# Hash attention into a gated product: inversions, bit transfers and the last pair's steps put in another order

## The chip, the cores and the metric

The kernel runs on one core of a Trainium2 chip. The metric is the device time of one execution in microseconds (us); of several runs the median is taken. A core has five engines that work side by side: TensorE (PE; its weight loads are shown apart as PEld), VectorE (DVE), ScalarE (ACT), GpSimd (POOL) and SyncE (SP). Each takes its instructions strictly in the order in which the program gives them, and semaphores tie the engines together. DMAs are issued by SP, ACT or POOL and land later.

## What is computed

The first half is attention with a mask by hash buckets, for 4 x 8 heads of 768 positions and 64 features; the second half takes the heads side by side as 3072 tokens of 512 features:

```python
q_bits, k_bits = (q @ proj > 0), (k @ proj > 0)        # 6 bits each
mask = bucket(q_bits) == bucket(k_bits)
scores = where(mask, q @ k.T / 8, -1e9)
attn = exp(scores - max); attn = attn / (sum(attn) + 1e-9)
x = attn @ v                                            # heads side by side: 3072 x 512
h = maximum(x @ w_in, 0)                                # w_in 512 x 2048
out = (h * h) @ w_out                                   # w_out 2048 x 512
```

The inputs come as 64-bit floats for the weights of the second half where the host gives them so; the kernel turns such words into 32-bit floats itself.

## The kernel before, in words

**Stages.** Heads are taken two at a time: 16 pairs, numbered 0 to 15, in the loop at L729. After the pairs comes a short seam (L858 to L873), then the product with `w_in`, the gate and the product with `w_out` for three chunks of 1024 tokens (from L1494). These products are split by Strassen's scheme (seven products for eight, twice nested in parts), so VectorE has many additions beside TensorE's work. `hidden` (L988) makes one unit of the first chunk: seven sums of four matmul instructions each in `product` (L890), with copies of partial results by ScalarE (`keep`, L904) and gates by VectorE (L985, L976). Its copies go to buffers of limited number, `KEPT` in L888: `two` has one.

**A pair.** The whole order is written out by hand (`tc.manual_schedule()`), so what stands first in the text stands first in each engine's queue. There are six key tiles of 128 keys and two halves of the queries. `score(pr, kt, i)` (L463) is a step of TensorE: matmuls of the hash bits (`bits`, bf16) that put a huge negative number where buckets differ, and matmuls of features (`feat`), in one of two PSUM tiles that are used in turn (`turn`, L103); ScalarE takes the exponential from it (`weight`, L458) into a ring of four tiles (`key_of`, L444). `attend(pr, kt, s)` (L513) multiplies such a tile with the values into the PSUM tile `xo`. Scores and attends alternate, and the attends of the last key tiles of a pair run beside the first scores of the next (`beside`). In `attend` the two halves of TensorE's rows write different banks; when they change over, `part` (L499) puts a fence between: a no-operation on POOL's queue that waits for the last matmul before and releases the first one after. The fence so waits behind whatever POOL has queued before it. A pair has such fences at `attend(pr, 0, 1)`, `attend(pr, 2, 0)` and `attend(pr, 4, 1)`; the last of these, here the fourth values' fence, falls into the next pair's start.

**Totals.** VectorE adds the six exponential tiles up (`add_up`, L485). TensorE sums over the keys by matmuls with ones (`sum_up`, L554, into PSUM tile `tot`), for two pairs together in each odd pair (`sums_and_hashes`, L581); the same place holds the hashes of the next two pairs (`hash_bits`, L373, and `signs`, L398, on ScalarE). VectorE then turns and inverts them (`invert`, L597: transpose, reciprocal, copy), ScalarE copies them across (`spread`, L613: four small copies), VectorE spreads them over the positions and scales the values (`normalize`, L620), and SP stores the result to DRAM. Before that, ScalarE has copied the values out of `xo` (`keep_x`, L535). An odd pair inverts for pair pr - 2, behind `add_up(pr, 1)` and `part_power`; an even pair inverts for pair pr - 2 near its start.

**Bits.** The signs of a pair are scaled on ScalarE (`weigh`, L405) and moved into place by eight DMAs on POOL's queue (`place_bits`, L412). Both stand in the middle of the pair before the one that needs them: `weigh` before `score(pr, 3, 0)` and `place_bits` behind `attend(pr, 0, 1)`.

**Weights.** Each pair also rounds one piece of the weights: `part_power` (VectorE), `place_power` (ScalarE, four small steps), `part_top` and `round_weight` (VectorE, two instructions each), then SP stores it. From pair 4 on some pairs add pieces of `w_in` for the later scheme (`sum_in`, L653), as many as L677 says, each with stores on SP.

**The start** fills TensorE with matmuls on nothing (`keep_busy`, L354) until the first inputs are there. **The seam** adds the last total, sums it, inverts, makes the subtractions of the first chunk (`sum_x`, L701), does the last values (`attend_whole`, L529) and normalizes.

Of the kernel before, what the change touches and what calls it, by code (L numbers as in the profile page):

```python
# [34 lines left out]
def kernel(  # L35
# [318 lines left out]
    def keep_busy(n):  # L354

        wide = busy.rearrange("p (o n) -> p o n", o=1).to_broadcast([P, 4, P])
        for _ in range(n):
            nc.tensor.matmul(
                out=void[:, 0].rearrange("p (o n) -> p o n", o=4), lhsT=busy, rhs=wide,
                start=True, stop=True,  # L360
            )
# [219 lines left out]
    def sums_and_hashes(prs, nexts):  # L581

        if not nexts:
            return sum_whole(prs)
        new_totals(prs)
        sum_up(prs[0], 0)
        for n, nxt in enumerate(nexts):
            hash_bits(nxt, turn("hash"))  # L590
            signs(nxt)
            if n < len(prs):
                sum_up(prs[n], 1)
            if n + 1 < len(prs):
                sum_up(prs[n + 1], 0)

    def invert(pr):  # L597

        flip = p_n.tile([P, HS], FP32, name="flip")
        nc.vector.transpose(  # L600
            out=flip.rearrange("p (c f) -> p c f", c=2), in_=spares.pop(pr)
        )
        once = p_n.tile([P, NB], FP32, name="once")
        nc.vector.reciprocal(
            out=once, in_=flip.rearrange("p (n f) -> p n f", f=32)[:, :, 0]
        )
        rec = p_n.tile([P, 2, NB], FP32, name="rec")
        nc.vector.tensor_copy(
            out=rec, in_=once.rearrange("p (o n) -> p o n", o=1).to_broadcast([P, 2, NB])
        )  # L610
        onces[pr] = once, rec
# [64 lines left out]
    for pr in range(NIN, NP):  # L676
        n = 1 + pr % 2  # L677
        sums[pr], todo = todo[:n], todo[n:]
# [29 lines left out]
    with tc.manual_schedule():  # L708
# [3 lines left out]
        keep_busy(6)  # L712
# [16 lines left out]
        for pr in range(NP):  # L729
# [12 lines left out]
            if pr == 0:  # L742
                first_score()
                first_keys(1, spare("hash"))
            else:
                score(pr, 0, 0)
                attend(old, 4, 0)
                score(pr, 0, 1)
                attend(old, 5, 0)
                add_up(old, SB - 1)  # L750
                if not odd:
                    invert(pr - 2)
                if pr == 1:
                    features(3)
                    part_top(0)
                round_weight(old)
                if later:
                    later.pop(0)()
                if more:
                    load_weight(pr + 1)  # L760
                for m in sums.get(pr, ()):
                    sum_in(m)
            score(pr, 1, 0)
            beside(4, 1)
            score(pr, 1, 1)
# [4 lines left out]
            else:  # L770
                keep_x(old)
                if odd:
                    sums_and_hashes(
                        range(max(pr - 2, 0), pr), [n for n in (pr + 1, pr + 2) if n < NP]
                    )
            add_up(pr, 1)
# [4 lines left out]
            part_power(pr)  # L781
            if odd and pr > 1:
# [3 lines left out]
            score(pr, 2, 0)  # L786
            if odd:
# [4 lines left out]
            if pr > 0:  # L792
                if pr > 1:
                    spread(pr - 2)
# [3 lines left out]
                if more:  # L798
                    weigh(pr + 1)
                else:  # L800
                    place_power(pr, 0, 0)
# [8 lines left out]
            if more:  # L810
# [11 lines left out]
            if not more:  # L822
                invert(old)
# [11 lines left out]
            if not more:  # L835
                spread(old)
                normalize(old)
# [4 lines left out]
            if 0 < pr < NP - 1:  # L842
# [14 lines left out]
            add_up(pr, 4)  # L857
        pr = NP - 1  # L858
        attend(pr, 2, 0)
        attend_whole(pr, SB - 2)  # L860
        add_up(pr, SB - 1)
        sum_whole((pr,))
        invert(pr)
        for n in (1, 2, 3):
            sum_x(0, n)
        spread(pr)
        attend_whole(pr, SB - 1)
        keep_x(pr)
# [873 lines left out]
```

## Time and profile before

| what | us |
|---|---|
| median of 3 runs | 860.38 (860.23 to 863.9) |
| the profiled execution | 860.77 |
| its span, first to last instruction | 859.2 |
| TensorE busy in the span | 849.3 (99%) |
| VectorE busy | 748.3 (87%) |
| ScalarE busy | 401.0 (47%) |
| GpSimd busy | 169.0 (20%) |

Times in the profile count from the span's start. The pairs run to about 321, the three chunks from there to the end. A row of the timeline gives start, duration, engine, line and operation, what is written and read, the number of instructions merged into the row, and in brackets the engine's idle time before it and what ended that. A busy TensorE need not be TensorE at its full clock: the granted clock is shown for each stretch. An engine that waits and is not needed costs nothing.

### The profile page before, as it was taken

The page shows a single profiled execution, that of the slowest core. Times are in us where ns is not written, and L with a number is a line of the kernel's source. Part 1 is how long each engine was busy: PE and PEld are TensorE (multiplying, and loading weights), DVE is VectorE, ACT ScalarE, POOL GpSimd, SP SyncE. Part 2 cuts the span into 40 slices and gives each one's busy share as a digit, 9 for nine tenths or more (in the row PEclk, how much of TensorE's full clock was granted, in tenths as well). Part 3 has the DMA queues.
Part 4 walks back from the last instruction along what each step waited for, and adds up shares of the span by engine and source line. Part 5 has one row for each costly group of instructions (what it writes and reads, how often), then busy time and mean ns, then how long its engine had stood idle before and what let it go on. Part 6 is the DMA issues. An engine that isn't in the chain of part 4 may idle for free.

```text
span 859.2 us, 17029 instructions
## 1 busy us (share of the span) xinstructions
PE 849.3 (99%) x6593; PEld 554.8 (65%) x6593; DVE 748.3 (87%) x1025; ACT 401.0 (47%) x752; POOL 169.0 (20%) x282
## 2 busy tenths in 40 slices
PE   8999999999999999999999999999999999999998
PEld 4555555555575544444688876667888766668886
DVE  5898999999999988988899978888988788889777
ACT  5887777778777752222111135554111255551111
POOL 1321111113231101653121221111000211100003
PEclk9999999999999999999999999999999999999999
DMA  9966998899996516999977995537647874335467
GB/s 214 169 122 146 179 187 192 190 186 230 273 219 205 168 63 221 326 282 288 352 244 241 265 216 180 176 123 250 221 148 185 184 241 164 133 114 166 141 172 146
DMA packets 234101, 170.13 MB, mean 198 GB/s; under 512 B 164712, under 2 KB 193200, under 8 KB 234016
## 3 DMA queue, kind: packets, MB, share of 16 engines
q1 hardware_dynamic: 194320, 87.78, 41.7%
q0 software_dynamic: 16512, 42.45, 16.0%
q10 hardware_dynamic: 23184, 38.78, 14.6%
q8 instruction: 53, 0.87, 0.4%
q14 instruction: 32, 0.26, 0.1%
HBM read 127.14 MB, written 41.16 MB: 196 GB/s over the span
## 4 chain that ended last, share of the span: by engine, by line
PE 84%; DVE 8%; ACT 3%; issue 2%; DMA 1%; POOL 0%; DVEq 0%; SPq 0%; ACTq 0%; POOLq 0%
PE acc L899 39%; PE acc L1163 13%; PE st L453 12%; PE xo L507 9%; PE acc L1116 8%; DVE t_x L495 2%; DVE total L495 1%; ACT e L459 1%; PE tot L564 1%; PE hash L382 1%; DMA out_dram<-h 1%; DMA bits<-signed 1%; DVE total L490 1%; DVE top L193 1%; DVE x_raw L630 0%
## 5 line engine op out<-in xcount | busy, mean ns | idle before, releaser
L459 ACT ACTIVATE e<-st 128x768 f32<-128x768 f32 x192 | 155.3, 810 | 60.4 <-PE st L453 57.8
L507 PE MATMUL xo<-e,v_nat 64*64 64x385 f32 (+1 forms) x1520 | 162.1, 485 | 0.0
L899 PE MATMUL acc<-b,leaf 128*128 128x256 f32 x600 | 133.0, 379 | 0.0
L899 PEld LDWEIGHTS acc<-b,leaf 128*128 128x128 f32 x600 | 113.9, 190 | 16.0 <-issue 0.5
L453 PE MATMUL st<-feat 64*64 64x384 f32 x1056 | 111.7, 483 | 0.1
L419 POOL DMA_DIRECT2D bits<-signed x120 | 62.8, 528 | 217.2 <-ACT signed L408 152.9
L507 PEld LDWEIGHTS xo<-e,v_nat 64*64 64x64 f32 (+1 forms) x1520 | 67.1, 133 | 57.8 <-issue 48.5
L1163 PE MATMUL acc<-t_x,w_unit 128*128 128x512 f32 x192 | 90.9, 595 | 0.0
L899 PE MATMUL acc<-t,leaf 128*128 128x256 f32 x336 | 75.9, 379 | 0.0
L453 PE MATMUL st<-bits 64*64 64x384 bf16 x768 | 70.4, 324 | 1.6 <-ACT e L459 1.0
L899 PEld LDWEIGHTS acc<-t,leaf 128*128 128x128 f32 x336 | 63.8, 190 | 8.7
L976 DVE SCALAR_TENSOR_TENSOR b<-h 128x512 f32<-128x512 f32 x96 | 65.7, 691 | 3.0
L495 DVE TENSOR_TENSOR total<-total,e 128x1536 f32<-128x1536 f32 x32 | 55.9, 1747 | 4.3 <-ACT e L459 3.9
L495 DVE TENSOR_TENSOR t_x<-t_x,e 128x1536 f32<-128x1536 f32 x32 | 55.8, 1745 | 2.9 <-ACT e L459 2.8
L453 PEld LDWEIGHTS st<-feat 64*64 64x64 f32 x1056 | 43.6, 133 | 20.5 <-issue 18.1
L899 PE MATMUL acc<-x,w_unit 128*128 128x512 f32 x128 | 56.5, 593 | 0.0
L453 PEld LDWEIGHTS <-bits 64*64 64x64 bf16 x768 | 29.8, 106 | 37.4 <-issue 34.6
L899 PE MATMUL acc<-b_t,leaf 128*128 128x256 f32 x240 | 53.8, 379 | 0.0
L906 ACT COPY two<-acc 128x256 f32<-128x256 f32 (+1 forms) x29 | 12.5, 431 | 87.5 <-PE acc L899 66.1
L1163 PEld LDWEIGHTS acc<-t_x,w_unit 128*128 128x128 f32 x192 | 35.8, 190 | 26.7 <-issue 23.0
L1284 POOL DMA_DIRECT2D out_dram<-h x24 | 15.6, 657 | 181.9 <-DVE h L1279 181.9
L453 PE MATMUL st<-t_x 64*64 64x384 f32 x480 | 50.6, 482 | 0.0
(189 smaller groups left out, 1371.0 us busy)
## 6 DMA issues: line engine op xcount, KB each, us to landing
leaf<-w_out ACTq DMA_DIRECT2D x142, 256.0 KB, 3.0
raw<-in_moe_w_in_dram SPq DMA_DIRECT2D x8, 1024.0 KB, 6.3
raw<-in_moe_w_out_dram SPq DMA_DIRECT2D x8, 1024.0 KB, 6.9
w_unit<-w_in SPq DMA_DIRECT2D x16, 512.0 KB, 4.0
w_unit<-w_in SPq DMA_DIRECT2D x8, 896.0 KB, 8.5
w_out<-sums POOLq DMA_DIRECT2D x16, 448.0 KB, 7.1
v_nat<-in_v_dram SPq DMA_DIRECT2D x16, 384.0 KB, 5.2
x_all<-x_raw SPq DMA_DIRECT2D x16, 384.0 KB, 3.2
```

Source lines behind the costliest of these rows:

```text
L193: nc.vector.scalar_tensor_tensor(out=one, in0=raw[:, :, :, 0], scalar=2.0**-32, in1=top, op0=ALU.mult, op1=ALU.add,)
L419: nc.gpsimd.dma_start(out=t[h * D:h * D + NBITS + 1, w, c * HS:(c + 1) * HS], in_=signed[pr % 2][at:at + NBITS + 1, h],)
L453: nc.tensor.matmul(out=st[k * HK:(k + 1) * HK, h, 0:HS], lhsT=src[1][rows, key], rhs=src[0][rows, cut], start=first, stop=not first, skip_ ...
L459: nc.scalar.activation(out=key_of(pr, kt)[:, :, i, 0:HS], in_=st[:, :, 0:HS], func=ACTF.Exp, scale=scale)
L495: nc.vector.tensor_tensor(out=totals[pr], in0=totals[pr], in1=e, op=ALU.add)
L507: return nc.tensor.matmul(out=outs[pr][h * D:(h + 1) * D, c, 0:HS + 1], lhsT=nat[pr, "v_nat"][rows, h, kt * D:(kt + 1) * D], rhs=key_of(pr ...
L899: nc.tensor.matmul(out=acc[to], lhsT=a(i), rhs=b(i), start=first and i == 0, stop=last and i == n - 1, skip_group_check=True,)
L906: nc.scalar.copy(out=t, in_=acc[of])
L976: nc.vector.scalar_tensor_tensor(out=out, in0=h, scalar=0.0, in1=h, op0=ALU.max, op1=ALU.mult)
L1116: nc.tensor.matmul(out=out, lhsT=w(a), rhs=b, start=start, stop=stop, skip_group_check=True)
L1163: nc.tensor.matmul(out=to, lhsT=w[:, PLACE[a], f], rhs=bt[b](f), start=first and f == 0, stop=last and f == NFT // 2 - 1, skip_group_check ...
L1284: queue.dma_start(out=out[at, m0 + a * 32:m0 + (a + 1) * 32].rearrange("(c i) j -> i c j", i=32), in_=ot[a * 32:(a + 1) * 32].rearrange("i ...
```

## The change

- In odd pairs from pair 5 on, `invert(pr - 2)` stands directly behind the block of totals and hashes, ahead of `add_up(pr, 1)`. `once` and `rec` get a second buffer.
- `spread(pr - 2)` stands behind `score(pr, 2, 0)` in place of behind `score(pr, 2, 1)`, in all pairs from 2 on.
- In even pairs from 2 on, `weigh(pr + 1)` stands behind the second score, and `place_bits(pr + 1)` behind `beside(4, 1)`, and so behind its fence. Odd pairs and pair 0 keep their places.
- In pair 1 the first hash and its signs stand ahead of `keep_x` and of the first half of the totals.
- In odd pairs `part_top` stands behind `add_up(pr, 4)`.
- Pairs 8 and 14 no longer have a `sum_in`, pair 15 has two.
- In pair 15 `part_power` and both inversions move forward (those of pairs 13 and 14), and the normalize of pair 14 moves into the seam. In the seam the last values stand ahead of the last totals, `keep_x` directly behind them, the inversion between the first and the second subtraction.
- `keep_busy` takes widths, and one matmul of half width is added.

```diff
--- before.py
+++ after.py
@@ -351,12 +351,12 @@
     busy = const.tile([P, P], BF16, name="busy")
     void = ps_o.tile([P, 2, 512], FP32, name="xo")
 
-    def keep_busy(n):
-
-        wide = busy.rearrange("p (o n) -> p o n", o=1).to_broadcast([P, 4, P])
-        for _ in range(n):
+    def keep_busy(*ns):
+
+        for n in ns:
             nc.tensor.matmul(
-                out=void[:, 0].rearrange("p (o n) -> p o n", o=4), lhsT=busy, rhs=wide,
+                out=void[:, 0, 0:n * P].rearrange("p (o n) -> p o n", o=n), lhsT=busy,
+                rhs=busy.rearrange("p (o n) -> p o n", o=1).to_broadcast([P, n, P]),
                 start=True, stop=True,
             )
 
@@ -583,16 +583,20 @@
 
 
         if not nexts:
+            keep_x(prs[-1])
             return sum_whole(prs)
         new_totals(prs)
-        sum_up(prs[0], 0)
-        for n, nxt in enumerate(nexts):
+        steps = [(pr, s) for pr in prs for s in range(2)]
+        if len(prs) > 1:
+            keep_x(prs[-1])
+            sum_up(*steps.pop(0))
+        for nxt in nexts:
             hash_bits(nxt, turn("hash"))
             signs(nxt)
-            if n < len(prs):
-                sum_up(prs[n], 1)
-            if n + 1 < len(prs):
-                sum_up(prs[n + 1], 0)
+            if len(prs) == 1 and nxt == nexts[0]:
+                keep_x(prs[0])
+            for _ in range(min(len(steps), len(prs))):
+                sum_up(*steps.pop(0))
 
     def invert(pr):
 
@@ -600,11 +604,11 @@
         nc.vector.transpose(
             out=flip.rearrange("p (c f) -> p c f", c=2), in_=spares.pop(pr)
         )
-        once = p_n.tile([P, NB], FP32, name="once")
+        once = p_n.tile([P, NB], FP32, name="once", bufs=2)
         nc.vector.reciprocal(
             out=once, in_=flip.rearrange("p (n f) -> p n f", f=32)[:, :, 0]
         )
-        rec = p_n.tile([P, 2, NB], FP32, name="rec")
+        rec = p_n.tile([P, 2, NB], FP32, name="rec", bufs=2)
         nc.vector.tensor_copy(
             out=rec, in_=once.rearrange("p (o n) -> p o n", o=1).to_broadcast([P, 2, NB])
         )
@@ -674,7 +678,7 @@
     todo = list(range(16))
     sums = {}
     for pr in range(NIN, NP):
-        n = 1 + pr % 2
+        n = 2 if pr % 2 else int(pr not in (NP // 2, NP - 2))
         sums[pr], todo = todo[:n], todo[n:]
 
     def load_x(i, fs=slice(0, NFT)):
@@ -709,7 +713,7 @@
         nc.gpsimd.memset(busy, 1.0)
         nc.vector.memset(projs, 0.0)
         load_first()
-        keep_busy(6)
+        keep_busy(4, 4, 4, 4, 4, 4, 2)
         make_identity(nc, ident)
         constants()
         load_pair(1)
@@ -747,6 +751,8 @@
                 attend(old, 4, 0)
                 score(pr, 0, 1)
                 attend(old, 5, 0)
+                if not odd:
+                    weigh(pr + 1)
                 add_up(old, SB - 1)
                 if not odd:
                     invert(pr - 2)
@@ -762,43 +768,53 @@
                     sum_in(m)
             score(pr, 1, 0)
             beside(4, 1)
+            if pr > 0 and not odd:
+                place_bits(pr + 1)
             score(pr, 1, 1)
             beside(5, 1)
             if pr == 0:
                 features(1)
                 load_pair(3)
             else:
-                keep_x(old)
                 if odd:
                     sums_and_hashes(
                         range(max(pr - 2, 0), pr), [n for n in (pr + 1, pr + 2) if n < NP]
                     )
+                    if not more:
+                        part_power(pr)
+                    if pr > NIN:
+                        invert(pr - 2)
+                else:
+                    keep_x(old)
             add_up(pr, 1)
 
 
             if pr in (X_0 + 1, X_0 + 2):
                 load_unit(pr - X_0 - 1)
-            part_power(pr)
-            if odd and pr > 1:
+            if more:
+                part_power(pr)
+            else:
+                invert(old)
+            if odd and 1 < pr < NIN:
                 invert(pr - 2)
             if pr == 0:
                 attend(pr, 0, 0)
             score(pr, 2, 0)
+            if pr > 1:
+                spread(pr - 2)
             if odd:
                 attend(pr, 0, 0)
             elif pr == 0:
                 attend(pr, 1, 0)
             score(pr, 2, 1)
             if pr > 0:
-                if pr > 1:
-                    spread(pr - 2)
                 if not odd:
                     attend(pr, 0, 0)
                 attend(pr, 1, 0)
-                if more:
+                if not more:
+                    place_power(pr, 0, 0)
+                elif odd:
                     weigh(pr + 1)
-                else:
-                    place_power(pr, 0, 0)
             else:
                 hash_bits(1, turn("hash"))
                 signs(1)
@@ -807,7 +823,7 @@
             if pr > 0:
                 place_power(pr, 0, int(not more))
             attend(pr, 0, 1)
-            if more:
+            if more and (odd or pr == 0):
                 place_bits(pr + 1, PARTS if pr else PARTS[:3])
             score(pr, 3, 1)
             attend(pr, 1, 1)
@@ -819,8 +835,6 @@
                     place_power(pr, 0, 1)
                 else:
                     place_power(pr, 1, 0)
-            if not more:
-                invert(old)
             add_up(pr, 3)
             if more:
                 load_values(pr + 1)
@@ -834,12 +848,11 @@
             attend(pr, 2, 1)
             if not more:
                 spread(old)
-                normalize(old)
             score(pr, 4, 1)
             if more:
                 place_power(pr, int(pr > 0), 1)
             attend(pr, 3, 1)
-            if 0 < pr < NP - 1:
+            if pr > 0 and more and not odd:
                 part_top(pr)
             score(pr, 5, 0)
             if pr == 0:
@@ -855,17 +868,21 @@
             if pr == 0:
                 place_power(0, 1, 1)
             add_up(pr, 4)
+            if odd and more:
+                part_top(pr)
         pr = NP - 1
         attend(pr, 2, 0)
         attend_whole(pr, SB - 2)
         add_up(pr, SB - 1)
+        attend_whole(pr, SB - 1)
         sum_whole((pr,))
+        keep_x(pr)
+        sum_x(0, 1)
         invert(pr)
-        for n in (1, 2, 3):
-            sum_x(0, n)
+        sum_x(0, 2)
+        sum_x(0, 3)
         spread(pr)
-        attend_whole(pr, SB - 1)
-        keep_x(pr)
+        normalize(old)
         normalize(pr)
         sum_x(0, 4)
         part_top(pr)
```

## The prediction

> **What bounds the kernel now.** I read the page's head and then one table of stretches, cut at the copies of finished values (L538), so that each stretch is one pair of heads long.
>
> ```profile
> span 859.2 us, 17029 instructions
> ```
>
> ```profile
> 71.23:91.70 20.47, 20.47 (x344) 11.24 (x332) 17.69 (x19) 15.67 (x25) 4.22 (x8) 1.00 0.68 150
> 109.15:130.05 20.90, 20.52 (x344) 11.30 (x332) 19.77 (x22) 15.68 (x25) 4.22 (x8) 1.00 0.94 195
> 130.05:147.50 17.45, 17.45 (x250) 9.55 (x248) 17.38 (x15) 13.99 (x23) 4.14 (x8) 1.00 0.81 178
> 147.50:168.42 20.92, 20.52 (x344) 11.26 (x332) 19.75 (x22) 15.68 (x26) 4.22 (x8) 1.00 0.95 205
> 185.87:206.65 20.78, 20.52 (x344) 11.26 (x332) 19.64 (x22) 15.67 (x26) 4.80 (x9) 1.00 0.93 228
> 206.65:224.71 18.06, 17.92 (x247) 10.85 (x246) 17.96 (x16) 13.99 (x24) 4.66 (x9) 1.00 0.99 237
> 224.71:245.45 20.74, 20.74 (x344) 12.37 (x332) 19.40 (x21) 15.68 (x26) 4.77 (x9) 1.00 1.04 240
> 262.90:283.44 20.54, 20.53 (x344) 11.40 (x332) 19.35 (x22) 15.66 (x25) 4.22 (x8) 1.00 0.61 189
> ```
>
> The columns are length, then busy time of PE, PEld, DVE, ACT and POOL, granted clock, DMA, GB/s. TensorE is full nearly everywhere, so only places where it waits or crawls can give time. A stretch that begins in an even pair takes 17.45 (130.05); the one of pair 10 took 18.06. A stretch that begins in an odd pair has the totals and hashes in it and takes 20.47 to 20.92, with the same 344 instructions: up to 0.45 of it is waiting. The timeline of pair 7 says for what, on VectorE, ScalarE and TensorE in turn:
>
> ```profile
> 149.96 0.69 DVE L647 TENSOR_TENSOR s_in<-s_in,in 128x512 f32<-128x512 f32 x1
> 150.56 1.75 DVE L490 SCALAR_TENSOR_TENSOR total<-e,e 128x1536 f32<-128x1536 f32 x1
> 152.23 0.69 DVE L149 TENSOR_SCALAR power<-raw 128x1024 uint32<-128x1024 uint32 x1
> 152.84 0.57 DVE L600 STREAM_TRANSPOSE flip<-tot 128x384 f32<-128x384 f32 x1
> 153.45 0.23 DVE L604 RECIPROCAL once<-flip 128x12 f32<-128x12 f32 x1
> 153.71 0.18 DVE L608 COPY rec<-once 128x24 f32<-128x24 f32 x1
> ```
>
> ```profile
> 152.65 0.81 ACT L459 ACTIVATE e<-st 128x768 f32<-128x768 f32 x1 [0.70 <-PE st L453]
> 153.93 0.83 ACT L618 COPY rec<-once 32x12 f32<-32x12 f32 x4 [0.46 <-DVE rec L608]
> 154.78 0.94 ACT L408 ACTIVATE signed<-signed,gains 128x768 bf16<-128x768 bf16 x1
> ```
>
> ```profile
> 156.47 0.36 PE L453 MATMUL st<-bits 64*64 64x384 bf16 x4 [0.40 <-ACT e L459]
> ```
>
> VectorE inverts late (152.84), ScalarE idles 0.46 for it, spreads, weighs, and only then takes the exponential whose PSUM bank the next score needs. The second place is the seam between attention and the gated product (two stretches, then VectorE, ScalarE, TensorE):
>
> ```profile
> 317.40:321.30 3.90, 3.87 (x24) 1.24 (x24) 2.52 (x5) 0.79 (x4) 0.00 (x0) 0.56 0.00 0
> 323.00:520.00 197.00, 197.00 (x672) 127.49 (x671) 173.28 (x263) 44.27 (x94) 58.21 (x75) 1.00 0.86 269
> ```
>
> ```profile
> 311.82 0.97 DVE L624 STREAM_TRANSPOSE recs<-rec 128x768 f32<-128x768 f32 x1
> 312.82 1.02 DVE L630 SCALAR_TENSOR_TENSOR x_raw<-x_raw,recs 128x768 f32<-128x768 f32 x1
> 313.76 3.61 DVE L495 TENSOR_TENSOR total<-total,e 128x1536 f32<-128x1536 f32 x2
> ```
>
> ```profile
> 311.74 2.22 ACT L459 ACTIVATE e<-st 128x768 f32<-128x768 f32 x3
> ```
>
> ```profile
> 312.49 2.91 PE L507 MATMUL xo<-e,v_nat 64*64 64x385 f32 x24
> 317.43 1.20 PE L564 MATMUL tot<-total,ones 128*32 128x192 f32 x16 [2.03 <-DVE total L495]
> 318.56 2.81 PE L507 MATMUL xo<-e,v_nat 128*64 128x385 f32 x8
> 321.30 3.27 PE L899 MATMUL acc<-x,w_unit 128*128 128x512 f32 x7
> ```
>
> TensorE waits 2.03 us for the last total (VectorE ends it at 317.37). In the stretch behind that wait the granted clock is 0.56 in place of 1.00, and the eight instructions of the last values take 2.81, nearly as long as the 24 before the wait (2.91). From 323 to 520 it is full again.
>
> **The change, part by part.** *Odd pairs.* From pair 5 on the inversion moves ahead of the total (1.75) and the power (0.69). In pair 7 it would start where the total does, at 150.56, and end 1.0 later (152.84 to 153.89), at 151.6. The spread now stands between two exponentials; the first ended at 151.95 (152.65 less 0.70), so it finds its input ready, by 0.35. Spread 0.83, exponential 0.81, weigh 0.94 and the next exponential 0.8 then run on end to 155.4, and the score wants the bank at 156.07 (156.47 less 0.40). So the wait goes, and late next would be that same exponential, with 0.7 to spare. Pair 3 keeps its inversion; only its spread moves. I take 20.40 as the floor of an odd stretch, 0.07 under the shortest seen: 0.07 + 0.50 + 0.52 + 0.38 + 0.34 + 0.14 = 1.95 for pairs 3, 5, 7, 9, 11, 13. Pair 1, whose first hash no longer waits for a total, I put at 0.05 (0 to 0.3). Bounds 0.9, if half the waits stay, to 2.4; taken 2.0.
>
> *Even pairs.* Weigh and its eight DMAs leave six us earlier. In pair 10 (POOL, the chain of waits, a weight load held by a fence, ScalarE):
>
> ```profile
> 211.18 4.11 POOL L419 DMA_DIRECT2D bits<-signed  x8 [11.18 <-ACT signed L408]
> ```
>
> ```profile
> 212.21 5.95 DMA bits<-signed
> ```
>
> ```profile
> 209.72 0.17 PEld L507 LDWEIGHTS xo<-e,v_nat 64*64 64x64 f32 x4 [0.15 <-POOLq L502]
> ```
>
> ```profile
> 203.03 0.81 ACT L459 ACTIVATE e<-st 128x768 f32<-128x768 f32 x1 [0.64 <-PE st L453]
> ```
>
> The bits landed at 218.2 (212.21 and 5.95), when pair 11 wanted them: 18.06 against 17.45, so 0.6 to gain (0 to 0.6). Weigh now follows the exponential of 203.03 and ends near 204.8, and POOL issues until 209.0 (4.11). Behind the eight DMAs on POOL's queue stands the fence of 209.72, which the next values on TensorE wait for: 0.7 to spare. ScalarE pays nothing, since it idles 0.64 before such exponentials and the same 0.94 leaves a fuller place. In odd pairs `part_top` goes behind the fourth total, VectorE work moved inside the pair: 0.
>
> *The seam.* Pair 14's inversion goes ahead of the later totals and its normalize (0.97 and 1.02) behind everything. From the start of pair 15's first total VectorE waited:
>
> ```profile
> 301.69 1.76 DVE L490 SCALAR_TENSOR_TENSOR total<-e,e 128x1536 f32<-128x1536 f32 x1 [1.72 <-ACT x_raw L538]
> ```
>
> It was free at 299.97. From there its new queue is: two input sums 1.3 (they came from pairs 8 and 14), power 0.7, inversion 1.0, total 1.75, inversion 1.0, total 1.75, normalize 2.0, total 1.75, which ends at 311.2. So the idle 1.72 hides the input sums; without it they would cost 1.3 here. Then VectorE waits for ScalarE's exponentials (311.74), which end the first near 312.0 as their spread comes sooner. Two totals, 3.5, end at 315.5 in place of 317.37. TensorE meanwhile: the fourth values begin near 313.9 (312.49, two attends of 0.65 and a turn) and last 1.3 (half of 2.81 less the drain); the last values follow at once to 316.5, their exponential done before 314.0. Totals take 0.7 (1.20, doubled by the clock). The product starts at 317.3 in place of 321.30: 4.0. No wait is left, and the product itself is late next. Were the total still done at 317.37, it would be 3.1; bounds 2.3 (clock, below) to 4.1.
>
> The Trainium skill, "TensorE: Matmul & The Clock Gate", section "HAM oscillation — how this bites in real kernels", has a rule against this: idle gaps over some 3.4 us cool the clock. By it the gap of 2.03 did not, and closing it returns no clock. The row with 0.56 right behind the gap says otherwise, and I follow the row.
>
> *Behind the seam.* TensorE starts four us sooner, VectorE does not: with the same subtractions, one normalize more and the same rounding it is free near 330.4, as now.
>
> ```profile
> 330.44 0.68 DVE L985 TENSOR_TENSOR h<-acc,one 128x512 f32<-128x512 f32 x1
> ```
>
> ```profile
> 346.79 0.68 DVE L985 TENSOR_TENSOR h<-acc,two 128x512 f32<-128x512 f32 x1
> ```
>
> ```profile
> w_unit<-w_in SPq DMA_DIRECT2D x8, 896.0 KB, 8.5
> ```
>
> A product is 28 instructions of 0.43 (3.27 for seven, with drain): 12.0. Begun at 317.3, the third wants to fill the single buffer `two` at 346.4; the add of 346.79 frees it at 347.5, and its copy is needed at 348.2. Its weights have 8.5 to land from an issue that waits for the rounding's store (330.4 and some three us), near 342, where it starts at 341.3. I take 0.2, bounds 0 to 1.5. After that VectorE's slack (197.0 less 173.3) lets it catch up. *Warm-up:* half a matmul more, 0.2, fits an idle gap:
>
> ```profile
> 2.49 1.48 PE L358 MATMUL xo<-busy 128*128 128x512 bf16 x3
> 4.39 3.58 PE L338 MATMUL tp<-ident,qk_nat 128*64 128x128 f32 x36 [0.41 <-POOL bits L268]
> ```
>
> So 0, and 0.2 if that cover were gone. The second buffers issue nothing.
>
> Sum: 2.0 + 0.6 + 4.0 - 0.2 = 6.4. The profiled execution took 860.77 (span 859.2 and 1.6 around it), which gives 854.4. It lies 0.4 above the median of the runs, 860.38, so the forecast is **854.0**.
>
> **The rivals.** *VectorE becomes the bound.* From 109.15 to 147.50 it is busy 37.15 of 38.35, and I ask for 37.85. If lag piles up there, most of the 2.0 and some of the seam stay away: 860.4 - 0.6 - 3.7 + 0.2 = 856.3. For it: 17.38 of 17.45 in an even stretch. Against: the work still fits. 0.13. *The seam's gain is given back behind it:* the third product waits 1.5 and the `w_out` stores pushed late 0.5 more: 855.8. 0.12. *The clock falls anyway*, for a cause other than the wait: half rate over some 3.4 us (318 to 321.3) costs 1.7 wherever it lies: 855.7. For it: one fall alone was seen. Against: it came with the longest wait. 0.10. By the skill's rule this is the case to expect. *Slower: POOL holds the fence.* If DMA issue in even pairs runs long or weigh comes late, the fence of 209.72 waits behind eight DMAs, and TensorE with it, in pairs 2 to 14. The price is seven times what goes beyond 0.7; from 1.6 late it eats all 6.4, and at 1.9 it gives 862.4. Against it: ScalarE waits for TensorE at that place, so weigh is on time. 0.05. *The change does little*, its waits come back one queue on: 859. 0.05.
>
> **How the numbers follow.** The forecast has 0.55, with bounds 852.7 to 855.3 (the seam and the odd pairs at their upper ends, or the odd pairs at their lower); the rivals as above. Three rivals end by 856.3, or 857.2 with the unknowns they share; beyond lie the last two, 0.10, and a little below. Range 852.6 to 857.2. About 0.5%, 4.3 us, is what a measurement of this kernel can tell from no change. Faster by that is under 856.1: the forecast whole, nearly all of the clock's case, half of the first two, 0.75. Within it 0.20, slower 0.05.
>
> **What would show it.** Odd stretches near 20.4, with ScalarE not waiting for `rec`; 17.45 for pair 10; at the seam a clock of 1.00 throughout, eight instructions of the last values in half of 2.81, totals straight behind, and the first product near 314.7 on the new trace (321.30 less 6.6). It would be wrong if TensorE waits for `bits` or a POOL fence, if the third product starts late, or if VectorE ends the last total after TensorE wants it.

## The result, and the profile after

Six executions of the changed kernel have a median of 853.9 us (853.43 to 855.45), six of the kernel before 860.31 (858.76 to 864.58). The ratio is 0.9917, with a 95% interval of 0.989 to 0.9944. The forecast was 854.0. The profiled execution took 854.06, and the head of its page gives the span, 6.7 under the 859.2 of before:

```profile
span 852.5 us, 17030 instructions
```

The table of stretches after the change has the columns of the prediction's first table: length, then PE, PEld, DVE, ACT and POOL, granted clock, DMA, GB/s. The cuts are the same copies of finished values.

```profile
107.85:128.18 20.33, 20.33 (x344) 10.12 (x332) 19.98 (x22) 16.58 (x27) 5.85 (x12) 1.00 0.93 192
128.18:145.63 17.45, 17.45 (x252) 8.07 (x248) 17.38 (x15) 13.46 (x23) 2.45 (x5) 1.00 0.87 188
203.73:221.18 17.45, 17.45 (x252) 8.07 (x248) 17.38 (x15) 13.45 (x23) 2.97 (x6) 1.00 0.99 255
312.00:317.00 5.00, 5.00 (x29) 2.23 (x26) 4.20 (x7) 2.18 (x6) 0.00 (x0) 1.00 0.00 0
323.00:520.00 197.00, 197.00 (x677) 128.25 (x676) 175.08 (x270) 46.13 (x100) 59.29 (x77) 1.00 0.86 272
```

The odd stretch is 20.33 long (it was 20.90), and TensorE's busy time is as long as the stretch: no wait is left in it. Pair 10's stretch (from 203.73) is 17.45, as pair 6's (from 128.18) is. From the last totals into the product (312 to 317) the granted clock is 1.00; behind the wait of before it was 0.56. In the profile of before, pair 10's stretch held a weight load of TensorE that waited 0.78 for the bits:

```profile
218.26 0.14 PEld L453 LDWEIGHTS <-bits 64*64 64x64 bf16 x2 [0.78 <-DMA bits<-signed]
```

Pair 7, after the change, on VectorE and then on ScalarE:

```profile
148.35 0.58 DVE L604 STREAM_TRANSPOSE flip<-tot 128x384 f32<-128x384 f32 x1
149.23 0.18 DVE L612 COPY rec<-once 128x24 f32<-128x24 f32 x1
149.32 1.75 DVE L490 SCALAR_TENSOR_TENSOR total<-e,e 128x1536 f32<-128x1536 f32 x1
```

```profile
150.08 0.83 ACT L622 COPY rec<-once 32x12 f32<-32x12 f32 x4
150.94 0.82 ACT L459 ACTIVATE e<-st 128x768 f32<-128x768 f32 x1
151.78 0.94 ACT L408 ACTIVATE signed<-signed,gains 128x768 bf16<-128x768 bf16 x1
```

The inversion stands ahead of the total and ends at 149.41, and the spread begins at 150.08 with no bracket: ScalarE did not wait for `rec`. The seam, TensorE and then VectorE:

```profile
308.32 4.21 PE L507 MATMUL xo<-e,v_nat 64*64 64x385 f32 x32
312.46 0.86 PE L564 MATMUL tot<-total,ones 128*32 128x192 f32 x16
313.24 3.70 PE L916 MATMUL acc<-x,w_unit 128*128 128x512 f32 x8
```

```profile
307.89 3.62 DVE L495 TENSOR_TENSOR total<-total,e 128x1536 f32<-128x1536 f32 x2 [0.83 <-ACT e L459]
```

The last total ends at 311.51, 0.95 before TensorE asks for it. Values, totals and product follow each other with no bracket at all.

Where the 6.7 of the span come from, stage by stage:

| stage | change in us |
|---|---|
| start, to the first score (10.10, now 9.12) | -1.0 |
| pair 1, from its first score to pair 2's copy (43.67, now 43.51) | -0.2 |
| the six odd stretches of pairs 3 to 13 (124.36 together, now 121.95) | -2.4 |
| pair 10 (18.06, now 17.45) | -0.6 |
| seam, from pair 15's copy at its start to the first product (20.41, now 16.51) | -3.9 |
| the products, to TensorE's last instruction (534.30, now 534.49) | +0.2 |
| the landing of the last stores (3.62, now 4.78) | +1.2 |

The odd stretches, pair 10 and the seam are the change, as the experiments show. Pair 1 has no experiment of its own, but it took 43.67 or 43.68 in all five profiles with its old order and 43.51 to 43.58 in all four with the new one. The products' 0.2 lies within chance (below). The first and the last row can be read from kernels that ran later. The start first: the 36 transposes in the changed kernel, in a kernel that differs from it only behind pair 1 (`f3_later_weigh`, below), and in one that has the old warm-up (`e2_odd_invert`):

```profile
4.43 2.55 PE L338 MATMUL tp<-ident,qk_nat 128*64 128x128 f32 x36 [0.24 <-POOL bits L268]
```

```profile
4.68 3.48 PE L338 MATMUL tp<-ident,qk_nat 128*64 128x128 f32 x36 [0.50 <-DMA qk_nat<-in_q_dram]
```

```profile
4.45 2.90 PE L338 MATMUL tp<-ident,qk_nat 128*64 128x128 f32 x36 [0.47 <-POOL bits L268]
```

The same 36 instructions take 2.55 and 3.48 with the same warm-up, and 2.90 with the old one (3.58 in the profile of before). The trace's record of the clock has it rise at 5.15, 7.28, 5.85 and 7.19 in these four executions, and each us of delay costs about half a us, whatever the kernel. So the start's 1.0 goes with the moment of the rise, and one warm-up alone has both 5.15 and 7.28: most likely it is chance. That the new warm-up has no part in it is not shown. Over all nine profiles of this kernel and its variants the rise came at 4.39, 4.94, 5.15 and 7.28 with it, and at 5.85 to 7.19 with the old one. The end is chance: in three kernels made from the changed one the last stores landed 3.46 to 3.65 after TensorE's last instruction, as before. Start and end nearly cancel.

### The profile page after: what moved, and what is told of

Its sections match the earlier page's. It is cut to its first block, busy times and chain, and to the rows that moved or that the text cites. A ratio compares the mean times of both kernels' runs of the same rounds, so it can differ in the third digit from the quotient of the medians.

```text
span 852.5 us, 17030 instructions
## 1 busy us (share of the span) xinstructions
PE 845.0 (99%) x6594; PEld 528.1 (62%) x6594; DVE 748.0 (88%) x1025; ACT 402.9 (47%) x752; POOL 168.1 (20%) x282
## 4 chain that ended last, share of the span: by engine, by line
PE 97%; DVE 1%; DMA 1%; POOL 0%; issue 0%; ACT 0%; SPq 0%; ACTq 0%; DVEq 0%; POOLq 0%
PE acc L916 39%; PE st L453 18%; PE xo L507 15%; PE acc L1180 13%; PE acc L1133 9%; PE tot L564 1%; PE hash L382 1%; DMA out_dram<-h 1%; POOL bits L268 0%; PE tp L338 0%; DVE h L1296 0%; DVE o L1282 0%; DVE tmp L1282 0%; DVE bits L433 0%; DVE sum L1282 0%
## 5 line engine op out<-in xcount | busy, mean ns | idle before, releaser
L507 PE MATMUL xo<-e,v_nat 64*64 64x385 f32 (+1 forms) x1520 | 155.1, 483 | 0.0
L453 PE MATMUL st<-feat 64*64 64x384 f32 x1056 | 107.9, 483 | 0.1
L507 PEld LDWEIGHTS xo<-e,v_nat 64*64 64x64 f32 (+1 forms) x1520 | 55.4, 133 | 68.6 <-issue 59.0
L453 PE MATMUL st<-bits 64*64 64x384 bf16 x768 | 64.4, 324 | 0.3 <-DVE bits L437 0.2
L453 PEld LDWEIGHTS st<-feat 64*64 64x64 f32 x1056 | 38.0, 133 | 27.5 <-issue 24.7
L916 PEld LDWEIGHTS acc<-b_t,leaf 128*128 128x128 f32 x240 | 45.6, 190 | 6.2
L923 ACT COPY one<-acc 128x256 f32<-128x256 f32 (+1 forms) x29 | 12.5, 432 | 77.6 <-PE acc L916 63.2
```

Source lines behind the costliest of these rows:

```text
L453: nc.tensor.matmul(out=st[k * HK:(k + 1) * HK, h, 0:HS], lhsT=src[1][rows, key], rhs=src[0][rows, cut], start=first, stop=not first, skip_ ...
L507: return nc.tensor.matmul(out=outs[pr][h * D:(h + 1) * D, c, 0:HS + 1], lhsT=nat[pr, "v_nat"][rows, h, kt * D:(kt + 1) * D], rhs=key_of(pr ...
L916: nc.tensor.matmul(out=acc[to], lhsT=a(i), rhs=b(i), start=first and i == 0, stop=last and i == n - 1, skip_group_check=True,)
L923: nc.scalar.copy(out=t, in_=acc[of])
```

## Theory and rivals

The theory is the prediction's: three separate waits go (odd pairs, pair 10, seam), and in the seam a halved clock with them. Its rivals: the halved clock has another cause than the wait; the order of values and totals matters by itself, not only VectorE's shorter queue; the place of the spread, not that of the inversion, gives the odd pairs' gain; and GpSimd's fence, behind eight DMAs, has no room. Four kernels put one part alone into the kernel before, three take one part out of the changed one, and one measures the clock by itself. Times of the first four stand against 31 executions of the kernel before (860.95), of the next three against 13 (859.73) on another chip. By the times alone, only `e2_odd_invert` of the first four is told apart from no change; for the other three the interval reaches 1 or passes it, and the traces carry the reading.

## The parts one by one, from the kernel before

**The values ahead of the totals, alone** (`e1_values_first`).

```diff
         add_up(pr, SB - 1)
+        attend_whole(pr, SB - 1)
         sum_whole((pr,))
+        keep_x(pr)
         invert(pr)
...
         spread(pr)
-        attend_whole(pr, SB - 1)
-        keep_x(pr)
         normalize(pr)
```

> The kernel before with one step of the seam moved: the last values (and the copy of the finished values) ahead of the last totals. Theory (the wait of 2.03 costs the clock): the last values start at 315.2 and end at 316.5, the total still ends at 317.37, so TensorE waits only 0.9; the granted clock stays 1.00, totals take 0.7 and the first product starts near 318.2 in place of 321.30, so 3.1 less, span near 856.1. Rival (the clock falls for another cause, as the rule of gaps over 3.4 us would have it): the half-rate stretch of 3.4 us stays, the step alone gives 1.4, first product near 319.9, span near 857.8.

Measured: 859.35, ratio 0.9986 (0.9971 to 1.0001), span 857.4. TensorE in its seam:

```profile
313.43 4.21 PE L507 MATMUL xo<-e,v_nat 64*64 64x385 f32 x32
318.46 0.86 PE L564 MATMUL tot<-total,ones 128*32 128x192 f32 x16 [0.83 <-DVE total L495]
319.25 3.70 PE L899 MATMUL acc<-x,w_unit 128*128 128x512 f32 x8
```

VectorE is as late as before, but the last values now lie in the wait, of which 0.83 is left, and the clock stays at 1.00: the eight instructions of the values no longer crawl. From the copy at the start of pair 15 (301.81) to the first product it is 17.44, where it was 20.41: 3.0 of the seam's 3.9, against a profile of before in which the clock fell. The span shows less, because another wait was longer in this execution, in pair 10 (a stretch of the same form):

```profile
206.16:225.58 19.42, 17.75 (x247) 11.03 (x247) 19.32 (x17) 14.00 (x24) 4.67 (x9) 1.00 0.92 230
```

19.42 where the profile of before had 18.06. Its start, on the other hand, was 0.5 shorter (first score at 9.58). Without both the span would be 856.5: the seam's 3.0 less 0.3 that it took longer behind the seam. That is the theory's side.

**The odd pairs, alone** (`e2_odd_invert`; the second buffers with it).

```diff
                         range(max(pr - 2, 0), pr), [n for n in (pr + 1, pr + 2) if n < NP]
                     )
+                    if NIN < pr and more:
+                        invert(pr - 2)
             add_up(pr, 1)
...
-            if odd and pr > 1:
+            if odd and (1 < pr < NIN or not more):
                 invert(pr - 2)
...
             score(pr, 2, 0)
+            if 1 < pr and more:
+                spread(pr - 2)
...
-                if pr > 1:
+                if not more:
                     spread(pr - 2)
```

> The kernel before with the odd pairs' part alone (pairs 5 to 13: inversion directly behind the block of totals and hashes, spread between the two exponentials, second buffers for once and rec); pair 15 and the seam as before. Theory: the stretches 20.90, 20.92, 20.78, 20.74, 20.54 all fall to 20.3 to 20.4, ScalarE no longer waits for rec, together 1.9 to 2.1 less, span near 857.2. Rival (VectorE is the bound): lag moves on, the stretches stay at 20.6 and above, under 1.0 less, span 858.3 or more. The seam keeps its wait of 2.0 and its clock near 0.56 in both.

Measured: 857.88, ratio 0.9964 (0.9949 to 0.9979), span 858.0. An odd stretch, pair 10's, and the 3.41 us of the seam after the wait:

```profile
146.17:166.50 20.33, 20.33 (x344) 10.12 (x332) 19.81 (x22) 15.88 (x26) 4.15 (x8) 1.00 1.00 200
204.27:223.62 19.35, 17.73 (x248) 9.88 (x244) 19.25 (x18) 14.01 (x23) 4.67 (x9) 1.00 0.93 229
316.47:319.88 3.41, 3.41 (x24) 0.99 (x12) 2.37 (x5) 0.80 (x4) 0.00 (x0) 0.50 0.00 0
```

All six odd stretches are 20.32 to 20.35, so this part alone gives the odd pairs' 2.3 to 2.4, with no help from `part_top` or the moved `sum_in`. Pair 10 waits 1.62 for its bits instead, and the seam's clock is halved as before. For pair 10 the row is:

```profile
217.39 0.47 PE L453 MATMUL st<-bits 64*64 64x384 bf16 x4 [1.62 <-DMA bits<-signed]
```

**The even pairs' bits, alone** (`e3_even_bits`).

```diff
                 attend(old, 5, 0)
+                if not odd:
+                    weigh(pr + 1)
...
             beside(4, 1)
+            if pr > 0 and not odd:
+                place_bits(pr + 1)
...
-                if more:
-                    weigh(pr + 1)
-                else:
+                if not more:
                     place_power(pr, 0, 0)
+                elif odd:
+                    weigh(pr + 1)
...
-            if more:
+            if more and (odd or pr == 0):
                 place_bits(pr + 1, PARTS if pr else PARTS[:3])
```

> The kernel before with the even pairs' part alone (weigh behind the second score, bit DMAs behind the fourth values' fence). Theory: the stretch of pair 10 falls from 18.06 to 17.45, the other even ones stay at 17.45, odd ones as before: 0.6 less, span near 858.6. Rival (POOL holds the fence): even stretches grow over 17.45, by seven times what the DMAs end late, and the weight loads of the first fence wait over 0.15 for POOL's queue.

Measured: 859.95, ratio 0.9985 (0.997 to 1.0), span 859.0. Pair 10 and the seam:

```profile
206.65:224.09 17.44, 17.44 (x247) 13.88 (x246) 17.37 (x15) 13.42 (x22) 2.95 (x6) 1.00 0.91 243
317.29:320.70 3.41, 3.41 (x21) 0.83 (x13) 2.58 (x5) 0.79 (x4) 0.00 (x0) 0.50 0.00 0
```

Pair 10's wait is gone. What it is worth is not one number: with the bits in their old place its stretch was 18.06, 19.42, 19.35 and 18.57 in four executions, 0.6 to 2.0 over 17.45; with the new place it was 17.39 to 17.45 in all five profiles. The price of 0.6 was that of one execution.

**Matmuls on nothing in the wait** (`e4_fill_wait`): all stays as it was, the wait is filled.

```diff
         add_up(pr, SB - 1)
+        nothing = turn("st")
+        for _ in range(9):
+            nc.tensor.matmul(out=nothing[:, 0]..., lhsT=busy, rhs=busy..., start=True, stop=True)
         sum_whole((pr,))
```

> The kernel before, unchanged in order, with nine matmuls on nothing (512 columns, bf16; result unused) put into the wait of the seam ahead of the last totals. It does no useful work sooner, so only the clock can give time. Theory (waiting costs the clock): the nine fill about 1.9 us from 315.3, the clock stays 1.00, the totals take 0.7 and the last values 1.3 in place of 2.81 with drain; first product near 319.5, 1.8 less, span near 857.4. Rival (the clock falls for another cause): the clock of that stretch stays near 0.56, first product at 321.3 or later, span 859.2 or more.

Measured: 860.47, ratio 0.9995 (0.998 to 1.001), span 857.8. TensorE in the seam:

```profile
315.74 2.12 PE L864 MATMUL st<-busy 128*128 128x512 bf16 x9
317.84 0.86 PE L564 MATMUL tot<-total,ones 128*32 128x192 f32 x16
318.62 1.52 PE L507 MATMUL xo<-e,v_nat 128*64 128x385 f32 x8
320.07 3.27 PE L906 MATMUL acc<-x,w_unit 128*128 128x512 f32 x7
```

Nothing is done earlier, yet the totals take 0.86 in place of 1.20 and the last values 1.52 in place of 2.81; the seam is 18.77, 1.6 shorter. This execution alone does not show that the filling kept the clock, though. Without the nine matmuls TensorE would have waited from 315.81 to 317.84. `g1_gaps` (below) finds that the clock changes only at fixed boundaries, 3.413 apart; one of them lies here at 316.61 (the first rise, 6.00, and 91 times 3.413). It would have cut the wait into 0.80 and 1.23, and waits that were cut like this did no harm in `g1_gaps`.

The median hardly moves. One reason stands in the executions of the kernel before: of the 44 in both sets, 21 show a mean granted clock of 0.998 or less, with a median of 861.4, and 23 of 0.999 or more, with 859.6. The clock falls in about half of the executions only. The other reason is that the seam is not the only place where it falls. Counted over all kernels:

| kernels | executions | at 0.998 or less |
|---|---|---|
| wait in the seam, bits in their old place (before, `e2_odd_invert`) | 54 | 27 |
| wait in the seam, bits in their new place (`e3_even_bits`) | 10 | 5 |
| wait filled or shortened, bits in their old place (`e1_values_first`, this one) | 20 | 7 |
| neither (the changed kernel and the three made from it) | 24 | 0 |

In the third row three of the seven are at 0.997; at 0.998 a late end of the last stores may have a part. Pair 10's waits are the likely cause, but in the profiles they are 1.67 at most, with the clock at 1.00 behind them. Where the clock fell in these seven is not shown.

## When a wait halves the clock

`g1_gaps` has no part of the kernel: bursts of matmuls, and between them one copy by ScalarE that the next burst needs.

```python
for n in range(6):
    for w in WIDTHS:                        # 128 to 2048 columns
        nc.scalar.activation(out=wide[:, 0:w], in_=acc[:, 2048 - w:2048], func=ACTF.Copy)
        for i in range(38 + 3 * n):
            nc.tensor.matmul(out=acc[:, 1536:2048], lhsT=wide[:, 0:P], rhs=one, ...)
```

> A kernel of its own that computes nothing of the reference (its output is zeros): bursts of 8 to 11 us of matmuls 128x512 in bf16, between which TensorE waits for one copy of ScalarE of 128 to 2048 columns, so waits of about 0.4 to 2.5 us, each length six times with other burst lengths. Theory: the granted clock is set at the ends of fixed stretches of 3.41 us, and a stretch idle for about half (1.7 us) or more halves the next one; then waits up to 1.6 never halve it, and longer ones do in a share of the cases that grows with their length and hangs on where the wait lies. Rival 1: every wait over some length between 0.8 and 2.0 us does, wherever it lies. Rival 2: none of these waits does, since only some 3.4 us of idleness would; the 0.5 in the seam had another cause.

Measured: 65 waits of 0.43 to 2.03 behind the clock's first rise. Stretches of its trace, length first, PE's busy time next, granted clock third from last: two waits, each with what follows it from the next boundary on, and then a third and its sequel.

```profile
335.15:337.18 2.03, 0.00 (x1) 0.01 (x1) 0.00 (x0) 1.88 (x1) 0.00 (x0) 1.00 0.00 0
337.73:341.14 3.41, 3.41 (x10) 1.22 (x8) 0.00 (x0) 0.00 (x0) 0.00 (x0) 0.50 0.00 0
...
600.62:602.65 2.03, 0.00 (x1) 0.00 (x1) 0.00 (x0) 1.88 (x1) 0.00 (x0) 1.00 0.00 0
603.97:607.38 3.41, 3.41 (x10) 1.21 (x9) 0.00 (x0) 0.00 (x0) 0.00 (x0) 0.50 0.00 0
```

```profile
101.21:103.24 2.03, 0.00 (x1) 0.00 (x1) 0.00 (x0) 1.88 (x1) 0.00 (x0) 1.00 0.00 0
103.24:106.70 3.46, 3.46 (x16) 1.58 (x17) 0.00 (x0) 0.00 (x0) 0.00 (x0) 1.00 0.00 0
```

The clock record holds four falls, each 3.41 long, at 337.73, 467.43, 603.97 and 747.33. Their distances from the first rise (6.63) are whole multiples of 3.413: the boundaries are fixed and do not follow the wait. The waits laid over this grid:

| longest idle time within one stretch of the grid | waits | halved |
|---|---|---|
| up to 1.71 | 58 | 0 |
| 1.82 to 1.86 | 3 | 0 |
| 2.03 | 4 | 4 |

Among those that halved nothing are two waits of 2.03, cut by a boundary into 0.99 and 1.04, and into 0.38 and 1.65. So the theory holds, with a limit between 1.86 and 2.03 (the 1.7 was too low); both rivals fall, the length alone does not decide, and 3.4 us of idleness are not needed. This also is what shows the cause of the halved clock in the seam: the wait of 2.03 lies whole within one stretch of the grid in the profiles of before, `e2_odd_invert` and `e3_even_bits`, and the clock falls at the end of that stretch each time.

The ends of two profiles narrow the limit. Here are the last stretch of the grid with work in it, and what follows, in `f3_later_weigh` and then in `e3_even_bits`:

```profile
846.96:850.37 3.41, 1.47 (x7) 0.77 (x5) 1.38 (x4) 0.27 (x1) 0.00 (x0) 1.00 0.52 79
850.37:852.60 2.23, 0.00 (x0) 0.00 (x0) 0.00 (x0) 0.00 (x0) 0.00 (x0) 0.50 0.27 76
```

```profile
853.19:856.60 3.41, 1.62 (x8) 0.90 (x6) 1.54 (x4) 0.27 (x1) 0.00 (x0) 1.00 0.58 90
856.60:859.00 2.40, 0.00 (x0) 0.00 (x0) 0.00 (x0) 0.00 (x0) 0.00 (x0) 1.00 0.26 72
```

In the first, 1.94 idle (a wait of 0.52, and 1.42 behind the last matmul) halves the next stretch; in the second 1.79 does not. So idle times within a stretch add up, and the limit lies between 1.86 and 1.94. For the kernel before, a wait of 2.03 then meets it in 46 to 50% of the positions: an estimate that takes all positions as equally likely. The 5 of 10 of `e3_even_bits` fit it; the 21 of 44 hold falls in other places too.

## Parts taken out of the changed kernel

**Last totals ahead of the last values again** (`f1_values_last`).

```diff
-        attend_whole(pr, SB - 1)
         sum_whole((pr,))
+        attend_whole(pr, SB - 1)
         keep_x(pr)
```

> The changed kernel with the last totals ahead of the last values again; all else as changed (VectorE's shorter queue stays). Theory: the last total now ends at about 311.5, and TensorE would ask for it about 0.6 earlier, so a wait of some 0.5 us comes back, the granted clock stays 1.00 in the seam, and the span grows by 0.3 to 0.6 to about 853.0. Rival: the order itself is what keeps TensorE and its clock going; then the wait is over 1.5 us, the clock is halved behind it and the span is 855.5 or more.

Measured: 853.9, ratio 0.9929 (0.9906 to 0.9953), span 851.2. TensorE:

```profile
308.00 2.91 PE L507 MATMUL xo<-e,v_nat 64*64 64x385 f32 x24
311.25 0.86 PE L564 MATMUL tot<-total,ones 128*32 128x192 f32 x16 [0.34 <-DVE total L495]
312.03 1.52 PE L507 MATMUL xo<-e,v_nat 128*64 128x385 f32 x8
313.48 3.70 PE L916 MATMUL acc<-x,w_unit 128*128 128x512 f32 x8
```

A wait of 0.34 comes back, the clock stays, and the seam is 17.07, 0.56 longer than in the changed kernel; the median of the runs is the same. So the theory's size is right, and the span is lower by chance alone: its clock rose at 4.39 in place of 5.15, and its stores landed 1.3 sooner. Either half of the seam's edit does most of the work: the new order alone brings 3.0, VectorE's shorter queue alone 3.3, both 3.9, each time against the profile of before with its fallen clock. Which of VectorE's moves (the inversions, the normalize, the input sums) shortens its queue most was not taken apart.

**The inversions of pairs 5 to 13 late, the spread early** (`f2_late_invert`).

```diff
-                    if pr > NIN:
+                    if not more:
                         invert(pr - 2)
...
-            if odd and 1 < pr < NIN:
+            if odd and 1 < pr < NP - 1:
                 invert(pr - 2)
```

> The changed kernel with the inversions of pairs 5 to 13 back behind the total and the power, while the spread keeps its new place between two exponentials. Theory: the copy that the spread waits for ends some 2.4 us later, ScalarE's next exponential waits behind the spread, and TensorE waits for the bank: 1.2 us more in each of five odd pairs, the stretches 20.33 become about 21.5, span near 858.5. Rival: the place of the spread gives the gain by itself and the inversion's place is hidden; then stretches of 20.3 and a span of 852.5.

Measured: 859.98, ratio 1.0001 (0.9989 to 1.0014), span 858.1. Pair 7's stretch, ScalarE and TensorE in it:

```profile
146.80:168.63 21.83, 20.72 (x344) 11.35 (x332) 19.73 (x22) 16.38 (x27) 5.82 (x12) 1.00 0.93 183
```

```profile
153.30 0.83 ACT L622 COPY rec<-once 32x12 f32<-32x12 f32 x4 [2.05 <-DVE rec L612]
154.15 0.81 ACT L459 ACTIVATE e<-st 128x768 f32<-128x768 f32 x1
```

```profile
155.01 0.36 PE L453 MATMUL st<-bits 64*64 64x384 bf16 x4 [1.10 <-ACT e L459]
```

Five stretches are 21.11 to 21.83 in place of 20.33, 6.5 together. ScalarE waits 2.05 for `rec` with a finished score behind it, and TensorE 1.10 for the bank. The early spread is no gain by itself; without the early inversion it costs more than the old order did.

**The even pairs' `weigh` one score later** (`f3_later_weigh`), the slower rival made to happen.

```diff
-                if not odd:
-                    weigh(pr + 1)
                 add_up(old, SB - 1)
...
             if pr > 0 and not odd:
+                weigh(pr + 1)
                 place_bits(pr + 1)
```

> The changed kernel with the even pairs' weigh one score later (behind the fourth values' fence and the exponential of 201.6 in pair 10), so that the eight DMAs end near 207.7 on GpSimd's queue where they ended at 206.15. Theory (the slower rival of the prediction, made to happen): the fence behind them comes 0.7 to 1.0 us later than TensorE wants it in each of seven even pairs, TensorE waits for POOL there, and the span grows by 5 to 7 to about 858.5. Rival: the fence has more room than that, nothing waits, span 852.5.

Measured: 853.79, ratio 0.9928 (0.9903 to 0.9953), span 852.6. GpSimd in pair 10, the weight load behind the fence, and pair 10's and pair 11's stretches:

```profile
204.68 4.10 POOL L419 DMA_DIRECT2D bits<-signed  x8 [7.02 <-ACT signed L408]
```

```profile
208.17 0.30 PEld L507 LDWEIGHTS xo<-e,v_nat 64*64 64x64 f32 x8 [0.35 <-POOLq L502]
```

```profile
204.98:222.37 17.39, 17.39 (x249) 8.12 (x249) 17.32 (x15) 13.40 (x23) 4.35 (x9) 1.00 0.95 246
222.37:242.76 20.39, 20.39 (x344) 10.20 (x332) 19.77 (x22) 16.57 (x27) 4.96 (x10) 1.00 1.06 246
```

The eight DMAs run 1.45 later than in the changed kernel, measured against TensorE's work, and the load behind the fence comes 0.17 late (0.35 idle where 0.18 is usual there). TensorE's matmuls show no wait; an even and an odd stretch together are 37.78 in both kernels (17.39 and 20.39, against 17.45 and 20.33). The theory falls: the fence had more room than 0.7. The load passes the fence at 208.17, while the row of the DMAs ends at 208.78, so the fence does not wait for the end of that row as the profile draws it. By these rows the fence would still be on time with the DMAs about 1.3 later than in the changed kernel (1.45 less 0.17, an estimate). How far they could slip before TensorE's matmuls wait was not tried.

## Why the prediction was right, step by step

- **Odd pairs**, 2.0 (0.9 to 2.4). The mechanism held as written: `rec` ready before the spread, the wait gone, nothing late next. The size was 2.4, and 2.6 with pair 1 (0.16 for 0.05), over the upper bound. The floor of 20.40 was mis-sized; all six stretches went to 20.33, and even the shortest, 20.47 with no idle time in its row, gave 0.15. Its weight loads were busy 11.24 and are 10.23 now, which suggests waiting that the row counts as work; this was not tried by itself.
- **Even pairs**, 0.6 (0 to 0.6). In the pair of profiles exactly 0.6. The upper bound was wrong: other executions had up to 2.0 to gain here. ScalarE paid nothing, as said.
- **The fence behind the eight DMAs**, 0.7 to spare. The room was larger: in `f3_later_weigh` 1.45 more delay cost TensorE's matmuls nothing. The rival's price was too high.
- **The seam**, 4.0 (2.3 to 4.1). 3.9 in the trace. VectorE's last total was to end 1.9 sooner (315.5 for 317.37). Measured from the copy at the start of pair 15 it ended 1.7 sooner (14.78 after it in place of 16.48). The totals were done in 0.86 and the product stood straight behind, as forecast. It began at 313.24, 1.5 ahead of the 314.7 given: 1.0 by the start, the rest by the pairs.
- **The clock in the seam**, taken as 1.00 against the rule. The Trainium skill, "TensorE: Matmul & The Clock Gate", section "HAM oscillation — how this bites in real kernels", warns of gaps over some 3.4 us. The runs show that shorter ones are enough: a wait of 2.03 whole within one stretch of 3.41 halved the clock in all seven places where one stood (four in `g1_gaps`, the seams of before, `e2_odd_invert` and `e3_even_bits`). What the step missed is that this 1.6 is paid in about half of the executions at most. The profile of before showed one that paid it. That the median still came out within 0.1 of the forecast is partly luck: the clock's 1.6 was counted in full, and against it the odd pairs gave 0.6 more than was taken and pair 10, which paid 0.6 in this profile, up to 2.0 in others.
- **Behind the seam**, -0.2 by the third product. Measured -0.2, but not shown to be that: the nine profiles range from 534.3 to 534.9 here, kernels without the change among them, so this is within chance, and the third product did not wait. The step's other half held: VectorE was free hardly sooner. From the copy at the start of pair 15 to its first gate it took 29.25 (296.73 to 325.98), before 29.55 (300.89 to 330.44).
- **Warm-up**, 0. The half matmul more does nothing that can be told from the clock's rise, which the start's 1.0 goes with; more is not shown.
- **VectorE as the bound**: it is busy 19.98 of 20.33 in an odd stretch and holds nobody up. The rival "does little" fell with the stretches.
- **The bounds of the forecast**, 852.7 to 855.3, do not follow from the ends that are named for them: the seam's and the odd pairs' upper ends give 853.5, the odd pairs' lower end 855.1. The measured 853.9 lies within both.

## What to carry to other kernels

When an instruction is moved between two that an engine must do on time, move its source first: the early spread gained 2.4 with the early inversion, and with the late one its five stretches took 4.2 more than in the kernel before (108.12 for 103.88). A wait's price is its length plus what it does to the clock, and that part may be paid in some executions only; so size it from several executions, not from the one that was profiled. One profile in which the clock stays up does not show that an edit kept it up, when it also stays up in half of the executions without the edit. When two edits close the same wait, each alone can be worth most of it (3.0 and 3.3 of 3.9 here), and their gains must not be added.

## What the runs showed of the hardware

TensorE's clock is decided at fixed boundaries 3.413 us apart: a stretch with 1.94 us idle or more halved the next one, a stretch with 1.86 or less did not, idle times within a stretch add up, and a wait that a boundary cuts can be harmless. The Trainium skill, "TensorE: Matmul & The Clock Gate", section "Part 1: The HAM clock gate (the "warmup" mystery)", has such a window of 3413 ns that runs on by itself; the record of `g1_gaps` agrees, with falls 97, 135, 175 and 217 times 3.413 behind the first rise. The first rise goes by the same grid. In the profiles it came between 4.39 and 7.28 after the span's start, and the first score at 8.79 to 10.30. Both ends of that range belong to kernels that are the same up to there, so the start alone can make executions of one kernel differ by 1.5 us.
